# First batch's softmax by column blocks, unread products between its loads, and norms straight after their scores, in a fused attention and gated feed-forward kernel

## The chip, the cores and the metric

One core of one Trainium2 chip. The time is device microseconds of an execution; lower is better. Each execution also leaves its span, from first to last instruction, which here is 2.0 to 2.4 us shorter than its time, and the mean clock granted to TensorE. All executions of this study count as fast (a single-core program has no slow die); where I call executions of one kernel slow below, I mean its longer ones.

## The reference

```python
# q, k, v: (4, 6016, 256) fp32; tau = 1
qn = q / (norm(q, axis=1) + 1e-6);  kn = k / (norm(k, axis=1) + 1e-6)
s = kn.transpose(0, 2, 1) @ qn / tau          # 256 x 256 for each batch
a = softmax(s)
x = (v @ a).reshape(24064, 256)
out = (sigmoid(x @ w_gate) * (x @ w_val)) @ w_out    # 256 -> 1536 -> 256
```

The attention matrix is only 256 x 256, so the kernel folds it into the weights: G = a @ w_gate and H = a @ w_val, once a batch ("folds", `gh`). Then v goes straight through G, H and w_out. To "evict" a product is to copy it out of PSUM, the memory into which TensorE writes. Batch n+1's scores, norms, softmax and folds run as side work inside batch n's stream. Only batch 0's stand alone, at the start.

## The kernel before

The start of batch 0: q and k arrive in 13 groups (eleven of 4 row tiles, one of 2, one of 1). For each, TensorE adds 256-column score products into `ps_s`, and one-column products of the squares into `ps_n`. Then softmax, four folds, and the stream, in which the other eight folds are spread.

```python
def busy(n):                                   # products that nobody reads
    ps = psg.tile([P, CH], FP32, tag="g", name="ps_busy")
    for _ in range(n):
        mm(ps[:, :P], ones_bf, ones_bf, True, True)

for g in range(last0 + 2):
    if g <= last0:
        t0, nt = groups0[g]
        sq[g] = (squares(0, t0, nt, 0, nc.vector),
                 squares(0, t0, nt, 1, nc.vector if g == last0 else nc.scalar))
        for u in range(nt):
            score(0, t0, u)
    if g >= 1:                                 # norms: one group late
        norm_mms(ps_n0, sq.pop(g - 1), groups0[g - 1][1], g == 1, g == last0 + 1)
norms_sqrt(0); nc.scalar.preload_act_table(ACT.Exp)
copy_s(0, 0); norms_inv(0); copy_s(0, 1)
busy(12); spread_k(0); busy(10)                # spread_k: 1/|k| along the free axis, into PSUM
scale_k(0)                                     # x *= rk, two of 128x256 on VectorE
transpose_v(0, 0, ...)                         # 8 TensorE transposes, one 128x1024 copy on VectorE
exps(0)                                        # two exps of 128x256, scale=r[:, j], on ScalarE
nc.scalar.preload_act_table(ACT.Sigmoid)
sums(0)                                        # row sums in one bank, add, reciprocal
for n in range(4):
    gh(0, n, ...)                              # evicted by VectorE and ScalarE in turn
# ...
for f in range(FC):                            # the stream, FC = 12 steps for each chunk of v
    glu(b, ci, f)                              # 2 ps_gate, 2 ps_val; sigmoid on ScalarE, hT on VectorE
    # ... output products of the chunk before, side work (for chunk 0: transpose_v(0, 1) at f == 7)
    if (b, ci) == (0, 0) and f < len(gh_order) - 4:
        gh(0, 4 + f, pso, "o", act=1)
```

## Time and profile before

The chain of waits is the path that ended last, followed back from the last instruction: at each step to what released it.

| what | value | where from |
|---|---|---|
| time, median of 3 | 832.22 us (832.06 to 832.91) | the times |
| the profiled execution | 834.39 us, span 832.2, clock 0.990 | its own row |
| TensorE busy | 813.7 us, 98% | part 1 of the page |
| idle before TensorE's instructions, all at the start | 18.5 us | span less busy |
| first ps_val / first ps_o | 42.25 / 57.86 us | chain of waits |

### The profile page before, as it was taken

The page shows a single profiled execution, that of the slowest core. Times are in us where ns is not written, and L with a number is a line of the kernel's source. Part 1 is how long each engine was busy: PE and PEld are TensorE (multiplying, and loading weights), DVE is VectorE, ACT ScalarE, POOL GpSimd, SP SyncE. Part 2 cuts the span into 40 slices and gives each one's busy share as a digit, 9 for nine tenths or more (in the row PEclk, how much of TensorE's full clock was granted, in tenths as well). Part 3 has the DMA queues.
Part 4 walks back from the last instruction along what each step waited for, and adds up shares of the span by engine and source line. Part 5 has one row for each costly group of instructions (what it writes and reads, how often), then busy time and mean ns, then how long its engine had stood idle before and what let it go on. Part 6 is the DMA issues. An engine that isn't in the chain of part 4 may idle for free.

```text
span 832.2 us, 13944 instructions
## 1 busy us (share of the span) xinstructions
PE 813.7 (98%) x5303; PEld 506.3 (61%) x5314; DVE 570.1 (69%) x977; ACT 391.1 (47%) x640; POOL 83.1 (10%) x159
## 2 busy tenths in 40 slices
PE   4899999999999999999999999999999999999998
PEld 4646666666666666665566666666566566666666
DVE  2367777777667777777757777777766666666664
ACT  4464444445644444444654444444555444444442
POOL 5532100002011100000220020000000000000000
PEclk9699999999999999999999999999999999999999
DMA  9999623335765543322973464323322424322211
GB/s 210 206 205 186 120 61 75 63 63 111 152 102 109 102 92 68 61 52 66 173 139 86 87 117 81 51 67 72 63 48 66 81 51 83 70 48 69 46 35 70
DMA packets 78738, 77.18 MB, mean 93 GB/s; under 512 B 50768, under 2 KB 55632, under 8 KB 78672
## 3 DMA queue, kind: packets, MB, share of 16 engines
q0 software_dynamic: 23920, 38.81, 28.0%
q1 hardware_dynamic: 54608, 36.97, 17.5%
q8 instruction: 41, 0.67, 0.3%
q10 hardware_dynamic: 144, 0.52, 0.2%
q14 instruction: 25, 0.20, 0.1%
HBM read 78.64 MB, written 24.64 MB: 124 GB/s over the span
## 4 chain that ended last, share of the span: by engine, by line
PE 95%; DMA 3%; ACT 0%; POOL 0%; issue 0%; DVE 0%; POOLq 0%
PE ps_o L88 30%; PE ps_val L88 29%; PE ps_gate L88 29%; PE ps_s L88 4%; DMA k_sb<-in_k_dram 3%; PE ps_gh L88 2%; PE ps_n L88 0%; ACT gh_H L335 0%; PE ps_busy L88 0%; ACT e_sb L288 0%; POOL q_sb L97 0%; PE ps_rk L88 0%; PE ps_tp L352 0%; POOL k_sb L97 0%; PE ps_r L88 0%
## 5 line engine op out<-in xcount | busy, mean ns | idle before, releaser
L380 DVE TENSOR_TENSOR hT<-ps_val,g_sb 128x512 bf16<-128x512 f32 (+1 forms) x576 | 391.7, 680 | 214.6 <-ACT g_sb L379 209.4
L379 ACT ACTIVATE g_sb<-ps_gate 128x512 bf16<-128x512 f32 (+1 forms) x576 | 338.4, 588 | 387.6 <-PE ps_gate L88 380.0
L88 PE MATMUL ps_val<-vT,gh_H 128*128 128x512 bf16 (+1 forms) x1152 | 338.1, 375 | 0.3
L88 PE MATMUL ps_gate<-vT,gh_G 128*128 128x512 bf16 (+1 forms) x1152 | 337.5, 375 | 0.2
L88 PE MATMUL ps_o<-w_out_sb,hT 128*128 128x256 bf16 x2256 | 326.2, 273 | 0.0
L88 PEld LDWEIGHTS <-hT 128*128 128x128 bf16 x2256 | 220.7, 98 | 124.7
L88 PEld LDWEIGHTS <-gh_H 128*128 128x128 bf16 x1152 | 112.7, 98 | 132.2 <-ACT gh_H L335 1.5
L88 PEld LDWEIGHTS <-gh_G 128*128 128x128 bf16 x1152 | 112.5, 98 | 37.4 <-ACT gh_G L335 0.3
L106 POOL DMA_DIRECT2D v_sb<-in_v_dram x48 | 25.5, 531 | 626.9 <-DMA vT<-v_sb 513.5
L406 DVE COPY out_sb<-ps_o 128x256 f32<-128x256 f32 x188 | 77.8, 414 | 13.9 <-PE ps_o L88 13.9
L88 PE MATMUL ps_s<-k_sb,q_sb 128*128 128x256 bf16 x376 | 72.2, 294 | 13.5 <-ACT k_sb L128 6.8
L88 PEld LDWEIGHTS <-q_sb 128*128 128x128 bf16 x376 | 38.9, 104 | 21.1 <-issue 7.5
L169 DVE TENSOR_TENSOR sq<-q_sb 128x1024 bf16<-128x1024 bf16 (+3 forms) x46 | 30.3, 662 | 20.8 <-PE ps_n L88 20.8
L207 DVE TENSOR_TENSOR acc<-acc,sq 128x1024 bf16<-128x1024 bf16 (+1 forms) x66 | 44.2, 670 | 0.0
L97 POOL DMA_DIRECT2D q_sb<-in_q_dram x48 | 26.5, 553 | 15.4 <-DMA q_sb<-in_q_dram 6.5
L97 POOL DMA_DIRECT2D k_sb<-in_k_dram x48 | 26.2, 546 | 13.2 <-DMA k_sb<-in_k_dram 8.4
L169 DVE TENSOR_TENSOR sq<-k_sb 128x1024 bf16<-128x1024 bf16 (+2 forms) x34 | 22.4, 658 | 0.0
L167 ACT ACTIVATE sq<-k_sb 128x1024 bf16<-128x1024 bf16 (+1 forms) x12 | 12.2, 1021 | 15.6 <-DMA k_sb<-in_k_dram 12.7
L88 PE MATMUL ps_gh<-w_val,e_sb 128*128 128x512 bf16 x44 | 13.2, 379 | 0.2
L88 PE MATMUL ps_gh<-w_gate,e_sb 128*128 128x512 bf16 x41 | 12.8, 379 | 0.2
L88 PEld LDWEIGHTS <-e_sb 128*128 128x128 bf16 x112 | 10.2, 98 | 4.4 <-ACT e_sb L288 0.7
L379 ACT ACT_TABLE_LOAD x6 | 7.7, 1283 | 9.2 <-PE ps_gate L88 9.1
(52 smaller groups left out, 106.7 us busy)
## 6 DMA issues: line engine op xcount, KB each, us to landing
out_dram<-out_sb SPq DMA_DIRECT2D x44, 512.0 KB, 2.9
v_sb<-in_v_dram POOLq DMA_DIRECT2D x44, 256.0 KB, 3.9
q_sb<-in_q_dram POOLq DMA_DIRECT2D x43, 256.0 KB, 6.5
k_sb<-in_k_dram POOLq DMA_DIRECT2D x43, 256.0 KB, 7.2
out_dram<-out_sb SPq DMA_DIRECT2D x4, 384.0 KB, 2.5
w_gate<-in_moe_w_gate_dram POOLq DMA_DIRECT2D x3, 256.0 KB, 6.8
w_val<-in_moe_w_val_dram POOLq DMA_DIRECT2D x3, 256.0 KB, 7.4
w_out_sb<-in_moe_w_out_dram POOLq DMA_DIRECT2D x1, 768.0 KB, 12.5
```

The source lines that it names most:

```text
L88: nc.tensor.matmul(out, lhsT=lhsT, rhs=rhs, start=start, stop=stop, **kw)
L97: nc.gpsimd.dma_start(out=tl[:, :nt, :], in_=rows(src, b)[:, t0 : t0 + nt, :])
L106: nc.gpsimd.dma_start(out=v_sb[:, :nt, :], in_=rows(v, b)[:, t0 : t0 + nt, :])
L167: nc.scalar.activation(out=sq[:, :nt, :], in_=src[:, :nt, :], func=ACT.Square)
L169: engine.tensor_tensor(out=sq[:, :nt, :], in0=src[:, :nt, :], in1=src[:, :nt, :], op=ALU.mult)
L207: nc.vector.tensor_tensor(out=acc[:, :nt, :], in0=acc[:, :nt, :], in1=st[b]["sq", w][:, :nt, :], op=ALU.add)
L379: nc.scalar.activation(out=g_sb[:, :n], in_=ps_gate[:, :n], func=ACT.Sigmoid)
L380: nc.vector.tensor_tensor(out=hts[b, ci][:, f, :n], in0=ps_val[:, :n], in1=g_sb[:, :n], op=ALU.mult)
L406: nc.vector.tensor_copy(out=out_sb[:, s, :], in_=ps)
```

## The change

Its intent: keep TensorE's clock up while loads trickle in, so that the tail after the last load runs at full clock; end the norms sooner; let one column block of the softmax run while the other is still scaled; have a fifth fold done before the stream.

```diff
+    busy(40)
+    for g, (t0, nt) in enumerate(groups0):
+        full = nt == TPC
+        engines = (nc.vector, nc.scalar) if g < last0 else (nc.scalar, nc.vector)
+        sq = [squares(0, t0, nt, w, engines[w]) for w in range(2)]
+        for u in range(nt):
+            score(0, t0, u)
+        if g == last0:
+            norm_mms(ps_n0, *held, False, False)
+        if full:
+            busy(6)
+        if g == last0 - 1:
+            held = (sq, nt)
+        else:
+            norm_mms(ps_n0, sq, nt, g == 0, g == last0, (0, 1) if g < last0 else (1, 0))
+        if full and t0 + nt < head:
+            busy(6)
# ... cut
-    busy(10)
-    scale_k(0)
-    exps(0)
-    nc.scalar.preload_act_table(ACT.Sigmoid)
-    sums(0)
-    for n in range(4):
-        gh(0, n, ...)
+    busy(4)
+    scale_k(0, 0); scale_k(0, 1)          # fused: x * r[:, j] * rk, four of 128x128
+    transpose_v(0, 0, ..., lambda *a: late.append(a))
+    exps(0, 0); exps(0, 1)                # one 128x256 for each column block, no scale operand
+    nc.scalar.copy(*late.pop())           # second half of vT
+    sums(0, 0)
+    gh(0, 0, psg, "g", act=False); gh(0, 1, psv, "v", act=True)
+    nc.scalar.preload_act_table(ACT.Sigmoid)
+    sums(0, 1, pss, "s")
+    gh(0, 2, ..., act=False); gh(0, 3, ..., act=False); gh(0, 4, pso, "o", act=True)
# gh_order: G and H of a block now stand together;  in the stream gh(0, 5 + f) in place of 4 + f
# transpose_v by TensorE: half of vT copied by VectorE, half by ScalarE, for chunk 1 too
# later batches: fused scales, two exps as before, sums_both in one bank as before
```

More of the change, by code (lines that the diff above doesn't have):

```diff
@@ L145, with invert @@
     st = {}
+    def invert(out, x, eps, num):
+        nc.vector.tensor_scalar(out=out, in0=x, scalar1=eps, scalar2=None, op0=ALU.add)
+        nc.vector.reciprocal(out, out)
     def score(b, t0, u):
@@ L172, in squares, with norm_mms @@
         return sq
-    def norm_mms(ps, sqs, nt, first, last):
-        for w, sq in enumerate(sqs):
+    def norm_mms(ps, sqs, nt, first, last, order=(0, 1)):
+        for w in order:
+            sq = sqs[w]
             for u in range(nt):
@@ L182, in norm_mms @@
                         ones_bf[:, 0:1],
-                        start=(first and w == 0 and u == 0 and j == 0),
+                        start=(first and w == order[0] and u == 0 and j == 0),
                         stop=(last and u == nt - 1),
@@ L215, in norms_mm @@
         ps = psm.tile([P, CB + C], FP32, tag="m", name="ps_n")
-        norm_mms(ps, (acc_q,), TPC, True, True)
+        norm_mms(ps, (acc_q,), TPC, True, True, (0,))
         for u in range(TPC):
@@ L240, in wide_scale @@
         for j in range(CB):
-            nc.vector.tensor_tensor(
-                out=s["x"][:, j, :], in0=s["s"][:, j, :], in1=s["rk"], op=ALU.mult
+            nc.vector.scalar_tensor_tensor(
+                out=s["x"][:, j, :],
+                in0=s["s"][:, j, :],
+                scalar=s["r"][:, j : j + 1],
+                in1=s["rk"],
+                op0=ALU.mult,
+                op1=ALU.mult,
             )
@@ L276, in copy_s, with scale_k, exps, sums @@
         nc.vector.tensor_copy(out=s["x"][:, j, :], in_=s["s"][:, j, :])
-    def scale_k(b):
+    def scale_k(b, i):
         s = st[b]
         for j in range(CB):
-            x = s["x"][:, j, :]
-            nc.vector.tensor_tensor(out=x, in0=x, in1=s["rk"], op=ALU.mult)
-    def exps(b):
-        s = st[b]
-        s["e"] = attp.tile([P, CB, C], BF16, tag="e", name="e_sb", bufs=2)
-        for j in range(CB):
-            nc.scalar.activation(
-                out=s["e"][:, j, :],
-                in_=s["x"][:, j, :],
-                func=ACT.Exp,
-                bias=shift,
-                scale=s["r"][:, j : j + 1],
-            )
-    def sums(b):
+            x = s["x"][:, j, ds(i * P, P)]
+            nc.vector.scalar_tensor_tensor(
+                out=x,
+                in0=x,
+                scalar=s["r"][:, j : j + 1],
+                in1=s["rk"][:, ds(i * P, P)],
+                op0=ALU.mult,
+                op1=ALU.mult,
+            )
+    def exps(b, i):
+        s = st[b]
+        e = attp.tile([P, CB, P], BF16, tag=f"e{i}", name=f"e_sb{i}", bufs=2)
+        nc.scalar.activation(
+            out=e, in_=s["x"][:, :, ds(i * P, P)], func=ACT.Exp, bias=shift
+        )
+        s.setdefault("e", []).append(e)
+        s.setdefault("rrow", [])
+    def sums(b, i, pl=psm, tag="m"):
+        s = st[b]
+        ps_r = pl.tile([P, 1], FP32, tag=tag, name="ps_r")
+        for j in range(CB):
+            mm(ps_r, s["e"][i][:, j, :], ones_bf[:, 0:1], j == 0, j == CB - 1)
+        r = attp.tile([P, 1], FP32, tag=f"rrow{i}", name="rrow", bufs=2)
+        invert(r, ps_r, 1e-9, 1.0)
+        s["rrow"].append(r)
+    def sums_both(b):
         s = st[b]
@@ L302, in sums @@
                     ps_r[:, i : i + 1],
-                    s["e"][:, j, ds(i * P, P)],
+                    s["e"][i][:, j, :],
                     ones_bf[:, 0:1],
@@ L309, in sums, with gh_tiles @@
         r = attp.tile([P, CB], FP32, tag="rrow", name="rrow", bufs=2)
-        nc.vector.tensor_scalar(out=r, in0=ps_r, scalar1=1e-9, scalar2=None, op0=ALU.add)
-        nc.vector.reciprocal(r, r)
-        s["rrow"] = r
-        s["gh"] = [
+        invert(r, ps_r, 1e-9, 1.0)
+        s["rrow"] = [r[:, i : i + 1] for i in range(CB)]
+    def gh_tiles(b):
+        st[b]["gh"] = [
             [ghpool.tile([P, CB, FG], BF16, tag=f"{n}{fg}", name=f"gh_{n}{fg}") for fg in range(NFG)]
@@ L316, in sums, with gh @@
         ]
-    gh_order = [(fg, w, i) for fg in range(NFG) for w in range(2) for i in range(CB)]
-    def gh(b, n, pl=None, tag=None, act=0):
+    gh_order = [(fg, w, i) for fg in range(NFG) for i in range(CB) for w in range(2)]
+    def gh(b, n, pl=None, tag=None, act=None):
         s = st[b]
@@ L326, in gh @@
                 ps,
-                s["e"][:, j, ds(i * P, P)],
+                s["e"][i][:, j, :],
                 w_sb[w][fg][:, j, :],
@@ L332, in gh @@
         dst = s["gh"][w][fg][:, i, :]
-        r = s["rrow"][:, i : i + 1]
-        if n % 2 == act:
+        r = s["rrow"][i]
+        if act if act is not None else n % 2 == 0:
             nc.scalar.activation(out=dst, in_=ps, func=ACT.Copy, scale=r)
@@ L340, with transpose_v @@
     vts = {}
-    def transpose_v(b, ci, ps=None):
+    def transpose_v(b, ci, ps=None, late=None):
         t0, nt = groups[ci]
@@ L354, in transpose_v @@
                 )
-            nc.vector.tensor_copy(out=vT[:, : nt * CB, :], in_=ps[:, : nt * CB, :])
+            half = nt * CB // 2
+            nc.vector.tensor_copy(out=vT[:, :half, :], in_=ps[:, :half, :])
+            (nc.scalar.copy if late is None else late)(vT[:, half : nt * CB, :], ps[:, half : nt * CB, :])
         vts[b, ci] = vT.rearrange("p (u cb) n -> p cb u n", cb=CB)
@@ L415, in busy @@
             mm(ps[:, :P], ones_bf, ones_bf, True, True)
+    busy(40)
     ps_n0 = psm.tile([P, 2 * CB], FP32, tag="m", name="ps_n")
-    sq = {}
     last0 = len(groups0) - 1
-    for g in range(last0 + 2):
-        if g <= last0:
-            t0, nt = groups0[g]
-            sq[g] = (
-                squares(0, t0, nt, 0, nc.vector),
-                squares(0, t0, nt, 1, nc.vector if g == last0 else nc.scalar),
-            )
-            for u in range(nt):
-                score(0, t0, u)
-        if g >= 1:
-            norm_mms(ps_n0, sq.pop(g - 1), groups0[g - 1][1], g == 1, g == last0 + 1)
+    for g, (t0, nt) in enumerate(groups0):
[14 more added lines that the diff above has]
+            busy(6)
     st[0]["n"] = ps_n0
@@ L438 @@
     spread_k(0)
-    busy(10)
-    scale_k(0)
-    transpose_v(0, 0, psv.tile([P, TPC * CB, P], BF16, tag="v", name="ps_tp"))
-    exps(0)
+    busy(4)
+    scale_k(0, 0)
+    scale_k(0, 1)
+    late = []
+    transpose_v(
+        0, 0, psv.tile([P, TPC * CB, P], BF16, tag="v", name="ps_tp"), lambda *a: late.append(a)
+    )
+    exps(0, 0)
+    exps(0, 1)
+    nc.scalar.copy(*late.pop())
+    gh_tiles(0)
+    sums(0, 0)
+    gh(0, 0, psg, "g", act=False)
+    gh(0, 1, psv, "v", act=True)
     nc.scalar.preload_act_table(ACT.Sigmoid)
-    sums(0)
-    for n in range(4):
-        gh(0, n, *((psg, "g"), (psv, "v"))[n % 2], act=1)
+    sums(0, 1, pss, "s")
+    gh(0, 2, psg, "g", act=False)
+    gh(0, 3, psv, "v", act=False)
+    gh(0, 4, pso, "o", act=True)
     def side_work(b):
@@ L484, in side_work @@
             (10, 0, wide_scale, n),
-            (10, 0, exps, n),
+            (10, 0, exps, n, 0),
+            (10, 0, exps, n, 1),
         ):
             side.setdefault((ci, FC + s), []).append((call[0], call[1:]))
-        at(11 * FC + 0, sums, n)
+        at(11 * FC + 0, sums_both, n)
+        at(11 * FC + 0, gh_tiles, n)
         for i in range(len(gh_order)):
@@ L505 @@
                     fn(*a)
-                if (b, ci) == (0, 0) and f < len(gh_order) - 4:
-                    gh(0, 4 + f, pso, "o", act=1)
+                if (b, ci) == (0, 0) and f < len(gh_order) - 5:
+                    gh(0, 5 + f, pso, "o")
             if prev is not None and block:
```

## The prediction

> **What bounds the kernel now.** I read the page first: its busy line gives TensorE (PE) 813.7 us of 832.2, 98%, VectorE (DVE) 69%, ScalarE (ACT) 47%. So for most of the span only fewer or faster matmuls could help. The strip of 40 slices (20.8 us each) shows where it is not so:
>
> ```profile
> PE   4899999999999999999999999999999999999998
> ...
> PEclk9699999999999999999999999999999999999999
> DMA  9999623335765543322973464323322424322211
> ```
>
> Only the first two slices have idle TensorE or a low clock, and there the DMA engines are full. The list of waits agrees: TensorE waits 6.8 us for the first cast of k, 6.6 us in eight waits for k loads, 0.3 us for an exp, and nothing after the start. The idle time is 832.2 - 813.7 = 18.5 us, all at the start. So I read the start: first the chain of waits between 30 and 48 us.
>
> ```profile
> 21.91 9.74 DMA k_sb<-in_k_dram
> ...
> 31.70 1.87 PE ps_s L88 x8
> ...
> 35.69 0.30 PE ps_n L88 x12
> 35.99 1.30 PE ps_busy L88 x12
> 37.29 0.92 PE ps_rk L88 x4
> 38.22 0.02 issue
> 38.24 0.43 DVE x_sb L282
> 38.67 0.02 issue
> 38.70 1.10 ACT e_sb L288 x2
> 39.80 0.05 issue
> 39.84 0.23 PE ps_r L88 x3
> ...
> 41.82 0.43 PE ps_gate L88 x2
> 42.25 0.74 PE ps_val L88 x2
> ...
> 47.34 0.70 ACT gh_H L335
> ```
>
> Until 31.7 us the path is loads of q and k. Then come the last scores, the norms, twelve unread products (ps_busy), the spread of the k norms, scaling, exp, row sums, the first folded weights (ps_gh), and at 41.82 the first gated product. In the stream after that a pair of 512-column matmuls takes 0.43 us in the chain; the first ps_val pair took 0.74, so 0.31 was a wait, and at 47.34 the stream waits for ScalarE to evict a gh_H tile that was made only just before its use. Second, the table of windows, whose columns are stretch, length, busy us of PE, PEld, DVE, ACT, POOL, then the clock:
>
> ```profile
> 16.50:17.00 0.50, 0.50 (x19) 0.49 (x17) 0.00 (x0) 0.32 (x1) 0.00 (x0) 1.00 1.08 205
> 17.50:18.00 0.50, 0.00 (x0) 0.00 (x0) 0.23 (x1) 0.00 (x0) 0.22 (x1) 0.54 1.18 217
> ...
> 32.00:37.00 5.00, 5.00 (x70) 4.16 (x69) 2.07 (x7) 2.40 (x4) 4.82 (x7) 0.50 1.22 206
> ```
>
> The clock falls to half near 17.5 us, is back from about 27.8 to 31 us, and is half again from 31.3 to 38 us: just the stretch that follows the last loads, where TensorE is on the path.
>
> **What the Trainium skill says.** "TensorE: Matmul & The Clock Gate", section "What's actually happening": the array runs at half rate until it has been busy for a window of about 3.4 us, and falls back after an idle window. The two rates agree (0.50 and 1.00; eight 256-column scores take 1.03 us warm, 1.86 cold). The idle window does not: from 10 us on no gap of TensorE is over 1.2 us, yet the clock falls. In this trace partial idleness (busy 0.8 to 1.1 of every 2 us between 12 and 18 us) is enough. "ScalarE: Activation LUTs", section "What ACT_TABLE_LOAD costs": a load is about 1283 ns plus a drain of about 1380 ns. The load agrees (1283 ns); the drain is not seen: the load that starts at 39.80 ends at 41.08 and the next activation starts at 41.10. The same section gives about 93 ns for each per-partition pointer operand, so exp without its scale pointer should fall from 592 to about 500 ns (an estimate from that page). "DMA: Bandwidth & Descriptors", section "Anatomy of one DMA — SWDGE (gpsimd) path", fits 2.0 us plus bytes over 436 GB/s, or 2.6 us for 256 KB; here such a load lands after 6.5 to 10 us, because the queue is full (about 207 GB/s).
>
> **The change part by part.** Landing times are start of issue plus time to landing, read load by load: last k load 27.17 + 6.5 = 33.67; first tile of w_gate 29.46 + 6.8 = 36.26, of w_val 30.67 + 6.8 = 37.47, second w_gate tile 31.94 + 6.8 = 38.74, second w_val 32.64 + 7.4 = 40.04. Nothing in the diff moves these issues; they do not wait for TensorE.
>
> (a) Unread products: 40 at the start, 6 after each full group's scores and 6 after its norms. Warm, a group is 8 scores (0.88), 6 products of about 0.055 (0.33), 16 norm products (0.44) and 6 more (0.33): 2.0 us in a period of about 2.5 us between loads, 80% busy where it was about 54%. Before the last load they lie in waiting time and cost nothing. I expect the clock to hold, and if it drops, the cold group is longer than its period, so TensorE would be fully busy and warm up again.
>
> (b) Norms follow at once instead of one group later. From 31.70 warm: scores of group 10 to 32.6, six products to 32.9, its norms (its k squares on ScalarE end at 32.8) to 33.4, scores of group 11 to 33.8, of group 12, whose k landed at 33.67, to 34.05, norms of both to about 34.4 (group 12's q square on ScalarE 33.7 to 34.1, its k square on DVE 33.75 to 34.05). Before: 35.99. **Gain 1.6.**
>
> (c) Square root 0.17, add, reciprocal: the old trace takes 0.6 us from norms to inverse (36.03 to 36.62), so 34.45 to about 35.1. The twelve products, 0.67 us warm, fit under that; cold they ended 0.5 us after the inverse. The spread took 1.11 us cold, about 0.6 warm: done at 35.75 against 38.22. **Gain so far 2.45.**
>
> (d) Softmax by column blocks. Old: first scale 0.43, two exps 1.10, sums. New: two fused scales of 128x128 (estimated 0.30 each, 0.24 apart, from 0.42 for 128x256) give block 0 at 36.3; its exp ends at about 36.9; sums and first fold at 37.1. Block 1's scales and exp (to 37.4) lie beside this. Then ScalarE copies half of vT (to about 38), evicts fold 1, loads the sigmoid table (38.8 to 40.1) and evicts fold 4 before the first sigmoid at 40.8 (before: 42.44). Fold 1 needs w_val at 37.47, almost exactly when it could start. DVE inverts twice and evicts folds 0, 2 and 3 at 0.75 each: 37.6 to 38.3, 38.7 to 39.4, 39.4 to 40.1. So the first gate starts at about 39.5 and the first ps_val at 40.1 against 42.25. **Gain 2.1**: DVE's serial evictions give back 0.35 us of (c).
>
> (e) Five folds stand before the gated stream, not four, so the fold matmuls in it are 7 pairs, not 8 (-0.43), and each weight group is complete one step earlier. The old stream from 41.82 to the first ps_o at 57.86 takes 16.04 us; its work is 24 pairs (10.37), 8 folds (3.46) and 8 transposes (0.45), 14.28. The difference 1.76 is the wait of 0.31 and two of 0.73 (at 47.3 and at 53.3). New: 39.5 + 10.37 + 3.03 + 0.45, and 0.2 for ps_val's wait, is 53.55. **Total gain 4.3.**
>
> (f) Later batches: instruction order on TensorE keeps its counts; two fused scales replace two multiplies of the same shape on an engine that is 69% busy; the sums stay in one bank. No TensorE wait stands there, so nothing to gain: 0.
>
> Sum: 832.2 - 4.3 = 827.9. I put 828.2, allowing for one more short wait.
>
> **Rivals.** *The clock stays cold after the last load.* Then the extra products are on the path: group 10 alone costs 1.87 + 0.64 + 0.5, norms end near 36, and (b) and (c) vanish; (d) and (e) leave about 2: 830. For it: the gate fell before with gaps of only 1.2 us. Against: 80% busy. One in five. *Weight loads become the bound*: with softmax earlier, folds 1 and 4 meet w_val at 37.47 and w_gate at 38.74. Slack is near zero for the first; a load later by 1 us costs up to 1. *The gain is given back later*: DMA stays full to about 78 us, and chunk 2 needs a vT whose transpose is issued at 49.52 and lands 15.5 later, at 65.0. Chunk 2 starts at about 74, or 70 after the change: 5 us of slack, so I expect no wait. *The serial chain on ScalarE or DVE* (table load between two evictions) could delay the first sigmoid; with two gate buffers a delay under 1 us should not stop TensorE.
>
> **Range and chances.** Warm and as worked: 827 to 829; cold or load-bound: 829.5 to 830.5. Range 826.9 to 830.2. A 2% gain would need 815.6, more than the path after the last load can give (from 33.67 to 41.8 is 8.2 us, and the waits in the stream 1.8); slower by 2% would need a wait in steady state, for which I see no cause. Faster 0.01, same 0.98, slower 0.01.
>
> **What would show it.** Clock 1.00 from 20 to 36 us (a); last norms near 34.4 (b); spread done near 35.8 (c); first ps_val near 40.1 (d); first ps_o near 53.5 and no wait of 0.7 us in that stream (e); TensorE without waits after 60 us, busy about the old figure plus the added products (f). Wrong if the clock is half at 32 to 36 us, if folds wait for w_val, or if a vT wait appears near 70 us.

## The result, and the profile after

832.48 us, median of 6 (832.20 to 832.73), against 832.41 for the kernel before in the same rounds (831.92 to 833.43). The ratio is 0.9999, interval 0.9986 to 1.0012. Ratios here are the mean time of one kernel's fast runs over that of the other's of the same rounds, so not quite the ratio of the medians quoted. The time is 4.3 us above the predicted 828.2 and above its range of 826.9 to 830.2.

The strip of the changed kernel's page shows the start better filled, and the load on the DMA engines as before:

```profile
PE   8899999999999999999999999999999999999998
...
PEclk9999999999999999999999999999999999999999
DMA  9999623236755543233974453223222324323211
```

Its window from 32 to 37 us, columns as before (length, busy of PE, PEld, DVE, ACT, POOL, then the clock):

```profile
32.00:37.00 5.00, 4.59 (x76) 4.25 (x75) 2.28 (x8) 3.39 (x5) 4.43 (x7) 1.00 1.22 206
```

The clock is full there, as planned. The chain of waits of the changed kernel, to lay beside the one in the prediction:

```profile
21.80 10.48 DMA k_sb<-in_k_dram
...
32.33 1.03 PE ps_s L88 x8
33.36 0.34 PE ps_busy L88 x6
...
34.75 0.28 PE ps_n L88 x12
35.03 0.69 PE ps_busy L88 x12
...
35.80 0.69 PE ps_rk L88 x4
...
36.52 0.62 DVE x_sb L293 x2
...
37.16 0.52 ACT e_sb L306
...
38.43 0.75 DVE gh_G L363
...
39.55 0.75 DVE gh_G L363
40.30 0.67 DVE gh_H L363
...
41.02 0.39 PE ps_val L88
...
52.35 0.61 ACT g_sb L407
...
52.98 0.70 DVE hT L408
...
53.73 0.59 PE ps_val L88 x2
...
56.05 0.44 PE ps_o L88 x4
```

The same line of the kernel before, in the profile that the prediction read:

```profile
57.86 0.44 PE ps_o L88 x4
```

The 41.02 is the second product of the first ps_val pair, the one that waits for fold 3. TensorE's own list shows the start of the pair:

```profile
40.58 0.82 PE L88 MATMUL ps_val<-vT,gh_H 128*128 128x512 bf16 x2
```

Norms end at 35.03, the spread at 36.50, the first ps_val pair starts at 40.58 (before: 42.25), and the first ps_o at 56.05. Against the first profile that is 1.81 us earlier, and the span is 1.8 us shorter, 830.4 against 832.2. After 60 us TensorE has no wait in either profile. So in the profiles the change gains 1.8 us, in the timed rounds nothing. Most of it isn't lost outside the span, as the times of the two profiled executions differ by 1.66 us too (834.39 and 832.73). So I asked whether the executions of one of the kernels differ among themselves.

### The profile page after: what moved, and what is told of

Read it like the earlier page. It is cut to its first block, busy times and chain, and to the rows that moved or that the text cites. A ratio compares the mean times of both kernels' runs of the same rounds, so it can differ in the third digit from the quotient of the medians.

```text
span 830.4 us, 14273 instructions
## 1 busy us (share of the span) xinstructions
PE 818.9 (99%) x5463; PEld 513.8 (62%) x5474; DVE 570.4 (69%) x981; ACT 390.8 (47%) x642; POOL 82.9 (10%) x159
## 4 chain that ended last, share of the span: by engine, by line
PE 95%; DMA 3%; DVE 1%; issue 0%; POOL 0%; ACT 0%; POOLq 0%; DVEq 0%; ACTq 0%
PE ps_o L88 30%; PE ps_gate L88 29%; PE ps_val L88 29%; PE ps_s L88 4%; DMA k_sb<-in_k_dram 3%; PE ps_gh L88 2%; PE ps_n L88 0%; DVE gh_G L363 0%; PE ps_busy L88 0%; POOL q_sb L97 0%; PE ps_r L88 0%; DVE hT L408 0%; PE ps_rk L88 0%; DVE gh_H L363 0%; DVE x_sb L293 0%
## 5 line engine op out<-in xcount | busy, mean ns | idle before, releaser
L88 PE MATMUL ps_s<-k_sb,q_sb 128*128 128x256 bf16 x376 | 66.8, 275 | 4.9 <-DMA k_sb<-in_k_dram 3.2
L88 PEld LDWEIGHTS <-q_sb 128*128 128x128 bf16 x376 | 36.8, 98 | 11.1 <-issue 4.5
L173 DVE TENSOR_TENSOR sq<-q_sb 128x1024 bf16<-128x1024 bf16 (+2 forms) x45 | 30.0, 669 | 18.5 <-DMA q_sb<-in_q_dram 10.7
L361 ACT ACTIVATE gh_G<-ps_gh,rrow 128x512 bf16<-128x512 f32 x22 | 15.1, 687 | 12.9 <-PE ps_gh L88 9.1
L363 DVE TENSOR_SCALAR gh_H<-ps_gh,rrow 128x512 bf16<-128x512 f32 x23 | 17.1, 743 | 1.6 <-PE ps_gh L88 1.6
L88 PE MATMUL ps_busy<-ones_bf 128*128 128x128 bf16 x182 | 16.6, 244 | 1.1 <-DVE shift L125 1.1
L88 PEld LDWEIGHTS <-ones_bf 128*128 128x128 bf16 x194 | 14.6, 110 | 1.5 <-DVE shift L125 1.1
```

The lines of the kernel that those rows point to most:

```text
L88: nc.tensor.matmul(out, lhsT=lhsT, rhs=rhs, start=start, stop=stop, **kw)
L173: engine.tensor_tensor(out=sq[:, :nt, :], in0=src[:, :nt, :], in1=src[:, :nt, :], op=ALU.mult)
L361: nc.scalar.activation(out=dst, in_=ps, func=ACT.Copy, scale=r)
L363: nc.vector.tensor_scalar(out=dst, in0=ps, scalar1=r, scalar2=None, op0=ALU.mult)
```

## The experiments

Twelve runs were made, all correct: the two kernels again, and nine edits of them. Spans are those of every execution of a kernel, the clock is its mean over the span. The kernel before averages 833.2 us in time over its 26 executions, the changed kernel 832.4 over its 11: of 1.0 us in span, 0.8 is left in time.

| kernel | executions | mean span | range | clock |
|---|---|---|---|---|
| before, all executions beside these runs | 26 | 831.0 | 829.8 to 832.4 | 0.987 to 0.994 |
| changed, first result | 6 | 830.1 | 829.8 to 830.4 | 0.998 to 1.000 |
| changed, again | 5 | 830.0 | 829.6 to 830.4 | 0.998 to 0.999 |
| before + products | 5 | 830.6 | 830.3 to 830.8 | 0.998 to 1.000 |
| before + products, groups 6 to 10 only | 5 | 830.5 | 830.2 to 830.7 | 0.991 to 0.996 |
| before + products + norm order | 6 | 830.25 | 829.9 to 830.6 | 0.998 to 1.000 |
| changed, no products between loads | 5 | 830.5 | 829.8 to 831.5 | 0.990 to 0.993 |
| changed, four folds ahead | 5 | 831.2 | 830.9 to 831.6 | 0.997 to 1.000 |
| changed, vT of chunk 1 by VectorE | 4 | 829.4 | 828.9 to 829.6 | 0.998 to 1.000 |
| the same, other evictions | 5 | 829.3 | 828.9 to 829.5 | 0.998 to 1.000 |
| the same, products in groups 6 to 10 only | 5 | 829.2 | 829.0 to 829.4 | 0.994 to 0.996 |
| whole softmax, five folds, vT by VectorE | 5 | 829.2 | 829.0 to 829.5 | 0.998 to 1.000 |

### 1. Is the first profile typical? Both kernels again

**Before, unchanged.**

> The kernel before, unchanged. Theory 1 (the first profile was an unusual execution: half clock just after the last loads, about 2 us lost): most executions have a span near 830.2 us, and a new profile shows the clock at 1.00 for most of 32 to 37 us, the last norms near 34.5 and the first ps_o about 2 us earlier than 57.86. Rival (the gain of the change is real in the span and is lost outside it): spans stay near 832.2 with the clock at 0.50 from 32 to 37 us while the time stays 832.4.

Time 833.43 (832.19 to 834.37); ratio 1.0 to itself. The profile caught 832.2 once more, clock 0.50 from 29.2 to 39 us, but the five spans are 832.2, 830.1, 830.0, 832.2 and 831.3. So neither theory's picture holds whole: the slow execution isn't rare, and the fast one isn't either.

**Changed, unchanged.**

> The changed kernel, unchanged. Both theories: span 829.8 to 830.5, first ps_o near 56 us, mean clock 0.998 or above. It shows how much of its start varies: the load of group 10's k landed at 32.3 us in its first profile against 31.65 in the profile before.

Time 832.19, spans 829.6 to 830.4, as expected. This time the ratio is 0.9987 (0.9973 to 1.0001), because the kernel before drew more slow executions beside it (median 833.47).

**Before, a third look.** Same file, no edit.

> The kernel before, a third time, for a profile. So far its executions had spans from 830.0 to 832.3 us, with mean clocks from 0.994 to 0.987, and both profiles caught 832.2. If this one is caught near 830: clock 1.00 in 32 to 36 us, spread done near 36.5 and first ps_o near 55.8, which would be the changed kernel's own figure (Theory 1). If at 832.2: half clock there once more.

It was caught at 830.3. Its window is here first, under it that of the second look (span 832.2):

```profile
32.00:37.00 5.00, 4.92 (x91) 4.55 (x89) 2.66 (x9) 3.29 (x5) 4.72 (x7) 1.00 1.22 205
```

```profile
32.00:37.00 5.00, 5.00 (x70) 4.21 (x68) 2.07 (x7) 2.40 (x4) 4.82 (x7) 0.50 1.22 206
```

The same program, once at full and once at half clock just after the last loads. The chain of the third look:

```profile
31.86 1.03 PE ps_s L88 x8
...
34.82 0.69 PE ps_busy L88 x12
...
35.59 0.70 PE ps_rk L88 x4
...
36.77 1.10 ACT e_sb L288 x2
...
40.32 0.74 PE ps_val L88 x2
...
55.93 0.44 PE ps_o L88 x4
```

Eight scores take 1.03 us, not 1.87; norms end at 34.82, the spread at 36.28, ps_val starts at 40.32, and the first ps_o at 55.93. Later loads are not the difference: group 10's k landed at 31.65 us in the slow profile, 31.81 in this one. The **unchanged** kernel, when its clock happens to be up, is at the first ps_o 0.12 us before the changed one. Of the 26 executions six have a clock of 0.987, and these six are all at 832.1 to 832.4. The fastest eight (829.8 to 830.2) have 0.991 to 0.993. In between the mean clock does not order them well: 831.5 occurs at 0.994, and the first profile had 0.990 at 832.2. The mean also counts cold stretches that cost nothing (see 2).

### 2. The products alone, and the change without them

```diff
 # before + products
+    busy(40)
             for u in range(nt):
                 score(0, t0, u)
+            if nt == TPC:
+                busy(6)
         if g >= 1:
             norm_mms(...)
+        if g <= last0 and nt == TPC and t0 + nt < head:
+            busy(6)
```

> The kernel before with only the unread products added (40 at the start, 6 after scores, 6 after norms of each full group). Theory 1: the clock is 1.00 from about 8 us to the end, and as most executions of the kernel before are warm after the last loads anyway, the time is within 0.5 us of it. Rival (cold tail is usual): about 1.5 to 2 us faster than the kernel before.

Time 832.82, ratio 0.9993 (0.9981 to 1.0006); spans 830.3 to 830.8, clock 0.998 or more. The slow executions are gone. Against the mean of the kernel before it gains 0.45 us, against its eight fastest executions it loses about 0.5. Why was not tested. Six products now stand ahead of the last norms, but in this profile TensorE was done with them and waited 0.17 us for group 11's k, which landed at 33.6 us, not at 33.1 as in the third look.

```diff
 # changed kernel, no products between loads
-    busy(40)
-        if full:
-            busy(6)
-        if full and t0 + nt < head:
-            busy(6)
```

> The changed kernel without the unread products of the loading groups (the 12 and 4 of the tail kept). Theory 1: the clock falls to 0.50 for part of 17 to 32 us as in the kernel before, at times also in the tail; time equal to the changed kernel or up to 1 us slower, with more spread. Rival: 1.5 to 2 us slower.

Time 832.34, ratio 0.9994; spans 829.8 to 831.5: the spread is back, with the best execution (829.8) near the best of the changed kernel (829.6). Its profiled execution (831.2) had a clock of 0.66 in 31 to 38 us, the scores at 1.86 us for eight and the first ps_o at 56.83.

To tie the spread to the clock of the tail and not to that of the whole start, I added the products around groups 6 to 10 only (the edit above with `g >= 6`, and no `busy(40)`).

> The kernel before with unread products only around groups 6 to 10, none earlier. Theory (the spread of the kernel before, spans 830.0 to 832.3, is the clock in 31 to 38 us alone; cold earlier costs nothing): clock half in part of 15 to 25 us, 1.00 from 31 us on, spans all within 830.0 to 830.8. It has fewer added instructions, so at most one more instruction fetch before the last loads; if that fetch is what makes group 10's k land at 32.2 instead of 31.65 in kernels with all products, it lands near 31.7 here. Rival (the spread has another cause): spans up to 832 in spite of a warm tail.

Time 832.82, ratio 1.0; spans 830.2 to 830.7. In its profile the clock is still half from 18.5 to 25 us and 1.00 from 31 to 38, its mean is 0.991 to 0.996, and no execution is slow. So here a cold clock while loads are awaited costs nothing that shows; the one after them does. Group 10's k landed at 31.46 us here, against 32.3 in the changed kernel. I took that for the delay by an extra instruction fetch; see run 5.

### 3. The norm order

The loop of the changed kernel, in the kernel before with the products.

> The kernel before with the unread products and the new order of the norms, nothing else. My working says that norms end 1.6 us earlier than in the cold profile; against the kernel with the products alone (span 830.3 to 830.8, norms at 35.2) it should save 0.3 us or less, because group 10's norms already were done before the last load landed. Rival: the norm order is worth 1 us or more by itself.

Time 832.18; mean span 830.25 against 830.58 with the products alone: 0.33 us (0.52 in time). Most of the 1.6 us of my working was clock, not order: the unchanged kernel's own norms end 1.17 us earlier in its fast execution (34.82 against 35.99).

### 4. The stream

```diff
 # changed kernel, v's second transpose
-            half = nt * CB // 2
+            half = nt * CB // 2 if late is not None else nt * CB
-            (nc.scalar.copy if late is None else late)(vT[:, half : nt * CB, :], ...)
+            if late is not None:
+                late(vT[:, half : nt * CB, :], ...)
```

> The changed kernel with the transpose of the second v chunk evicted whole by VectorE as before, not half by ScalarE. In the changed kernel's profile the half copy (0.58 us on ScalarE at 51.87) delays the sigmoid of step 8, and TensorE loses about 0.8 us to 54.3. If that copy is what took back the gain of the earlier folds, this is 0.6 to 0.8 us faster than the changed kernel (span near 829.3); if the loss was there anyway, equal.

Time 831.83, ratio 0.9981 (0.9967 to 0.9994). Mean span 829.4, 0.7 us below the changed kernel: as the first theory expected. In the changed kernel ScalarE's order and TensorE's matmuls stand so:

```profile
51.87 0.58 ACT L383 COPY vT<-ps_tp 128x512 bf16<-128x512 bf16 x1 [1.20 <-DVE vT L382]
52.35 1.09 ACT L407 ACTIVATE g_sb<-ps_gate 128x512 bf16<-128x512 f32 x2
```

```profile
52.05 0.59 PE L88 MATMUL ps_val<-vT,gh_H 128*128 128x512 bf16 x2
53.00 0.59 PE L88 MATMUL ps_gate<-vT,gh_G 128*128 128x512 bf16 x2 [0.36 <-ACT g_sb L407]
53.73 0.59 PE L88 MATMUL ps_val<-vT,gh_H 128*128 128x512 bf16 x2
```

and without the half copy:

```profile
52.01 0.59 PE L88 MATMUL ps_val<-vT,gh_H 128*128 128x512 bf16 x2
52.44 0.59 PE L88 MATMUL ps_gate<-vT,gh_G 128*128 128x512 bf16 x2
52.87 0.59 PE L88 MATMUL ps_val<-vT,gh_H 128*128 128x512 bf16 x2
```

The half copy waits 1.20 us for VectorE's half, holds up two sigmoids, and TensorE, with two gate buffers, waits. A start-to-start step of 0.43 becomes 0.95 and then 0.73. Moving this copy, 0.58 us on ScalarE, away from VectorE cost 0.7 us on TensorE.

```diff
 # changed kernel, four folds ahead of the stream
-    gh(0, 4, pso, "o", act=True)
-    if (b, ci) == (0, 0) and f < len(gh_order) - 5:
-        gh(0, 5 + f, pso, "o")
+    if (b, ci) == (0, 0) and f < len(gh_order) - 4:
+        gh(0, 4 + f, pso, "o")
```

> The changed kernel with four folds ahead of the gated stream and eight in it, as before. My working gave the fifth fold 0.43 us plus two waits of 0.73. If it is worth that: 1.5 to 1.9 us slower than the changed kernel. If the waits were 0.31 each, as the ends of the matmuls say, 0.4 to 1.1 us slower. Rival: it takes nothing, since ScalarE's table load sets the first sigmoid anyway: equal.

Time 833.29, ratio 1.0003; mean span 831.2, 1.15 us above the changed kernel. The fifth fold is worth 1.15: more than 0.4 to 1.1, far less than the 1.5 to 1.9 that two waits of 0.73 would give. In the new fold order the last fold of a group is VectorE's, and TensorE waited 0.71 and 0.59 us for it.

### 5. Column blocks, evictions, and a better version

```diff
 # on top of v's second transpose by VectorE
-    nc.scalar.preload_act_table(ACT.Sigmoid)
     sums(0, 1, pss, "s")
     gh(0, 2, psg, "g", act=False)
-    gh(0, 3, psv, "v", act=False)
-    gh(0, 4, pso, "o", act=True)
+    gh(0, 3, psv, "v", act=True)
+    nc.scalar.preload_act_table(ACT.Sigmoid)
+    gh(0, 4, pso, "o", act=False)
```

> The changed kernel with v's second transpose evicted by VectorE alone, fold 3 evicted by ScalarE and fold 4 by VectorE, the sigmoid table loaded after fold 3. If VectorE's three evictions in a row set the first ps_val (41.0 us): ps_val at about 40.3, span 0.5 to 0.7 us below the run with the transpose alone changed (829.4), so near 828.8. Rival (the table load sets the pace): the sigmoid moves later by as much and nothing is gained.

Time 831.74, ratio 0.9986; mean span 829.3 against 829.4: nothing. A miss, and the rival was right. The product of ps_val that waits for fold 3 started at 40.7, not 41.0, but the first sigmoid moved from 41.4 to 41.7, behind the table load, and TensorE lost 0.2 us at 43.5 (first ps_o 55.12 against 55.19).

The same with products around groups 6 to 10 only:

> The same, with unread products only around groups 6 to 10. If the instruction fetches of the added products delay group 10's k by 0.6 us: span 0.3 to 0.6 us lower still, near 828.4. If the last k load (33.6 us in all kernels so far) is what counts: equal.

Time 831.44, ratio 0.9985; mean span 829.2: equal within the noise. Group 10's k landed at 32.1 although instructions were fewer. **My theory of the instruction fetches falls**: in the run that follows all the products are there and it landed at 31.65.

```diff
 # whole softmax again, on top of v's second transpose by VectorE (in short, not line by line)
+    busy(6)
+    two tensor_tensor 128x256 (x *= rk); transpose_v whole on VectorE
+    two exps with scale=r[:, j]; preload Sigmoid; sums_both(0)
+    gh(0, 0..4): VectorE, ScalarE, VectorE, ScalarE, VectorE
-    scale_k by blocks, exps by blocks, sums by blocks, half of vT on ScalarE
```

> The changed kernel with the first batch's softmax whole again (two scalings, two exps with the scale in them, sums in one bank, table load straight after the exps), five folds, new fold order, v's second transpose on VectorE. It takes the column blocks alone away. If column blocks are worth the 0.5 us by which the first exp ends earlier: 0.3 to 0.7 us slower than the run with column blocks and the same evictions. If VectorE's and ScalarE's queue behind them takes it back: equal within 0.3 us.

Time 831.21, ratio 0.9983 (0.9969 to 0.9997); mean span 829.2, against 829.3 with column blocks and the same evictions of the folds. In time it is 0.3 us faster (means 831.27 and 831.56). The **column blocks, with the table load where this kernel has it, gain nothing** within 0.3 us. With whole blocks the first exp ends later, but ScalarE's table load follows the exps at once, and the first sigmoid starts at 40.37 instead of 41.69. So the run did not take the column blocks alone away, as I had written, but with them the place of the table load and the half copy of vT, and it has six more unread products. Column blocks with the load straight after their exps were not tried. This version beats both kernels: its spans, 829.0 to 829.5, lie below all of the changed kernel's (829.6 to 830.4, from other rounds) and all of the 26 of the kernel before. It is still the same time within 2%.

What stays open is why group 10's k lands at 31.5 to 31.9 us in some profiles and at 32.1 to 32.3 in others, what decides whether an execution is at half clock after its last loads, and why time minus span differs between kernels (1.99 to 2.35 us).

## Why the prediction was wrong

The steps, in its own letters:

- **What bounds the kernel now**: the place was right, the size wrong. The step that failed is the sentence that the clock "is half again from 31.3 to 38 us", taken as a property of the kernel. It was a property of that execution. In a fast execution the chain is already at 34.82 for the norms, 36.28 for the spread and 55.93 for the first ps_o. Of the 2.45 us of (b) and (c), 1.94 was this (38.22 less 36.28). The hint was in the table: the profiled execution took 834.39, the timed ones 832.06 to 832.91.
- **The sum**: it takes a gain read in that long execution from 832.2, which is its span, and gives the rest as a time. From its time the same gain leads to 834.39 - 4.3 = 830.1. So 2.2 us of the miss lie here, and the other half in a gain of 4.3 where the profiled pair shows 1.7 in time.
- **(a)** right in the main: with all the products the clock is 1.00 from 12 us on in every profile (in two it was 0.50 from 8 to 11 us, among the first scores), and its value is that the slow executions vanish. Averaged over executions that is about 0.5 us.
- **(b)** predicted 34.4, measured 35.03. Group 10's k landed 0.63 us later than in the profile that I used, and so did all that follows. By itself the norm order gives 0.33.
- **(c)** 35.75 predicted, 36.50 measured: the same 0.63, and 0.1 more.
- **(d)** from the spread to the first ps_val pair 4.35 us predicted, 4.08 measured (36.50 to 40.58), against 4.03 before: near. That it gains nothing of its own was right: VectorE's three evictions, one after the other, stand in the chain from 38.43 to 40.97. The run with the whole softmax says the same.
- **(e)** failed twice. *A miscount*: from 41.82 to the first ps_o at 57.86 there are 26 pairs of gate and value matmuls, not 24, since ps_o follows the first step of the next chunk. The work is 11.22 + 3.46 + 0.45 = 15.13, so the waits were 0.91 us, three of about 0.31, and not 1.76. The chain misled me: where it steps over to ScalarE for 0.70 us, a gate pair runs beside it on TensorE, unseen. *A wait left out*: the half copy on ScalarE, 0.8 us in that profile, 0.7 us by experiment. I had listed the half copy of chunk 0 in (d), and forgotten that of chunk 1, at step 8 of the stream.
- **(f)** right: no wait of TensorE after 60 us.

The sum for the profiled pair: 4.3 less 0.86 (miscount), 0.63 (later load), 0.8 (half copy) and 0.2 (small delays, what is left over) is 1.8, as measured. From there to the timed rounds: the kernel before averages 831.0 in span, not 832.2, the changed kernel 830.05. A mean gain of 1.0 us in span, 0.8 in time, is below what six executions of a kernel that ranges over 2.6 us can show. That the first rounds showed no gain at all was luck: the six of the kernel before average 832.5 us there, its 26 later ones 833.2.

Of the rivals, *cold after the last load* was meant for the changed kernel and did not come true there; it describes the slow executions of the kernel before. *Weight loads* and *vT near 70 us* did not appear. *The serial chain on ScalarE* did, at the place where I had not looked: a copy of 0.58 us stopped TensorE in spite of two gate buffers. (The 2.6 us that the prediction gives for a 256 KB load is an estimate from the page's fit; nothing rests on it.)

## What to carry to other kernels

Before working from one profile, compare that execution's own time with the timed ones; where the difference is as large as the effect you reckon with, take a second profile. A chain of waits shows one path and hides what runs beside it: to size a wait, count the work between two marks, and check it against the start times on the engine itself. Moving a short copy to an engine that feeds a double-buffered stage can cost the bound engine more than the copy lasts.

## What the Trainium skill lacked or had wrong

- "TensorE: Matmul & The Clock Gate", section "What's actually happening", has the clock fall after an idle window of about 3.4 us. Here it fell with no gap of TensorE over 1.2 us, after stretches with TensorE busy for 0.8 to 1.1 of every 2 us; at 79 to 88% busy it held (16 to 24 and 24 to 31 us: 1.00 in the profiles with all the products). The page's section "A second HAM failure mode: psum-queue depth-cycling" does tell of a clock that swings through frequent short idle times, but gives no busy share.
- The section "What's actually happening" also says that the window is free-running, that the number of slow matmuls at the start varies by run, and that the warm-up costs under 1% of a typical span. The runs show a size for a whole kernel, 829.8 to 832.4 us for one program, 0.3%; they don't show the window itself. The section speaks of the kernel's start; it lacks that the clock can differ from run to run later too, here after the last loads (first ps_o at 57.86 or 55.93 us).
- "ScalarE: Activation LUTs", section "What ACT_TABLE_LOAD costs": the 1283 ns are right; the drain of about 1380 ns is not seen, as the next activation starts 0.02 us after the load (39.80 + 1.28 to 41.10). Its 93 ns for a pointer operand is near: exp of 128x256 took 592 ns with the scale operand and 507 without.
- No page that I read tells what delays a 256 KB load in a full queue by 0.6 us now and then (group 10's k: 31.5 to 32.3 us). The runs don't settle it.
